# First token tiles of a fused attention and expert kernel: zeros stored later, experts prepared before the first keys, kv products and query copies a tile or two on

## Chip, cores and metric

The kernel runs on one core of a Trainium2 chip. The metric is the device time of one execution in microseconds (us), with the median of several runs as the value. Before the change the median of 3 runs is 1384.82 us.

## What is computed

Three layers follow each other on 4608 tokens of 512 values (8 batches of 576 tokens, 8 heads of 64): a linear attention with a root mean square norm, a mixture of 8 experts of which each token uses one, and a layer with a cosine gate. All of it is float32.

```python
kv = np.einsum('bhsd,bhse->bhde', k, v)
out = np.einsum('bhsd,bhde->bhse', q, kv)
rms = np.sqrt(np.mean(out * out, axis=-1, keepdims=True) + 1e-06)
x = (out / rms * g_norm)                       # then (4608, 512)
xn = x / (norm(x) + 1e-06); en = expert_emb / (norm(expert_emb) + 1e-06)
logits = xn @ en.T / tau                       # argmax picks the expert
out[mask] = gate_w[mask, None] * (np.maximum(x[mask] @ w1[e], 0.0) @ w2[e])
h = out @ w_in                                 # second layer
y = (h * np.cos(h)) @ w_out
```

## The kernel before

The order of the instructions on each engine is the order in which the code is written: there is no planner. Three stages run one after the other. The first, some 146 us long, makes the attention in 36 tiles of 128 tokens, finds each token's expert and scatters the rows to the expert's place in DRAM. The second runs the experts in chunks of 304 tokens, the third the last layer in blocks of 512 tokens. Only the first stage is touched.

**Loads.** SP's queue loads, batch by batch, `km`, `vm` (1 MB each), their remainders `kr`, `vr` and the queries `qm` (`load_kv`, `load_q`, L520 to L542). ScalarE's queue loads the embeddings, the temperature and the gain twice: `g2` by partitions and `g_bc` as a row on all partitions (L557 to L561). Behind them it stores four blocks of zeros, `none`, to columns 304 to 511 of `yT` (L581, 104 KB each). VectorE squares the gain row in place (L597); that step stands ahead of the steps of `prepare_experts` on VectorE. The loads share eight completion semaphores in turn: a load waits until the transfer that had its semaphore before is complete.

**A batch's kv.** `kv_pair(b, hp)` multiplies keys and values of two heads (L650, L653), with the copy to `kvb` after the fourth pair (L657). `kv_transpose` turns the four results on TensorE and copies them (L665, L667). `kv_logits` multiplies them by `gz`, the normed expert embeddings, and copies 16 columns per pair beside them (L673, L677). `prepare_experts` makes `gz` (L620 to L637): square, root and scaling of the embeddings on ScalarE and VectorE, four transposes on TensorE (L634).

**A tile.** `emit_out(t)` multiplies the turned queries `qT` by `kvb` (L706) and `emit_square(t)` squares the result on ScalarE (L716). `emit_root(t - 1)` takes a logarithm and an exponential of the tile before (L722, L723). `q_by_rows(b, half)` copies half of a batch's queries in another order on ScalarE (L616), and `emit_qT(t + 2)` turns the queries of the tile after the next on TensorE (L694) and copies them on ScalarE (L696); there is one PSUM buffer for that. Then come the kv steps of later batches that the tables `due_first` (tiles 0 to 8) and `due` name, in which (1, "t") is the transpose and (1, "z") the logits of the next batch but one half, and last the scaling on VectorE (L757). A batch has 4.5 tiles: tiles 0 to 3 are batch 0, 4 to 7 batch 1, and tile 8 holds the remainders of both.

**Spins.** `spin(n)` runs n products of a matrix of ones into an unused PSUM tile (L855), each in two instructions, to keep TensorE at work.

Of the kernel before, what the change touches and what calls it, by code (L numbers as in the profile page):

```python
# [19 lines left out]
B, H, S, D = 8, 8, 576, 64  # L20
# [5 lines left out]
NTILE = NT // 128  # L26
# [3 lines left out]
CH = 304  # L30
# [6 lines left out]
def tile_kernel(ctx, tc, q, k, v, g_norm, emb, tau, w1, w2, w_in, w_out, out):  # L37
    nc = tc.nc
# [6 lines left out]
    yT = dram.tile([DM, NT + CH], F32, name="yT")  # L45
# [450 lines left out]
    if True:  # L496
# [80 lines left out]

        none = ca.tile([128, 512 - CH], F32, name="none")
        nc.gpsimd.memset(none, 0.0)
        for d in range(4):  # L580
            nc.scalar.dma_start(out=yT[d * 128:(d + 1) * 128, CH:512], in_=none)  # L581
        nums = ca.tile([128, 4, 9], I32, name="nums")
        nc.gpsimd.iota(out=nums[:, :, 0:8], pattern=[[2 * S, 4], [S, 2], [1, 4]], base=0, channel_multiplier=4)
        for i in range(2):
# [57 lines left out]
        def kv_pair(b, hp):  # L642
            if hp == 0:
                kvp_t[b] = ps_s.tile([128, 4, 128], F32, name="kvp", tag="kvp")
            p, dst = kvp_t[b], kvb[b % 3]
            rr = slice(32 * (b % 4), 32 * (b % 4) + 32)
            ho = [(2 * hp + n, p[64 * n:64 * n + 64, hp, 0:D]) for n in range(2)]
            for r in range(4):
                for h, o in ho:
                    nc.tensor.matmul(out=o, lhsT=km[b][:, h, r, :], rhs=vm[b][:, h, r, :], start=(r == 0), stop=False)  # L650
            for r in range(2):
                for h, o in ho:
                    nc.tensor.matmul(out=o, lhsT=kr[rr, h, r, :], rhs=vr[rr, h, r, :], start=False, stop=(r == 1))  # L653
            if hp == 3:
                for n in range(2):
                    r = slice(64 * n, 64 * n + 64)
                    nc.scalar.activation(out=dst[r, :, n * D:(n + 1) * D], in_=p[r, :, 0:D], func=ACTF.Copy)  # L657
# [24 lines left out]
        def where(t):  # L682
            j, i = divmod(t, 9)
            return j, (2 * j + i // 4 if i < 8 else None), i % 4
# [168 lines left out]
        def spin(n):  # L853
            for i in range(n):
                nc.tensor.matmul(out=warm[:, 0, 0:128], lhsT=ones, rhs=ones, start=True, stop=True)  # L855

        spin(24)
        load_kv(1)
        load_q(1)
        load_kv(2)  # L860
        for hp in range(2):
            kv_pair(0, hp)
        prepare_experts()
        kv_pair(0, 2)
        q_by_rows(0, 0)
        kv_pair(0, 3)
        spin(5)
        emit_qT(0)
        spin(4)
        emit_qT(1)  # L870
        kv_transpose(0)
        q_by_rows(0, 1)
        spin(5)
        kv_logits(0)
        spin(2)

        due = {0: [(1, 2), (1, 3)], 1: [(1, "t")], 2: [(1, "z")], 3: [(2, 0), (2, 1)], 4: [(2, 2)], 5: [(2, 3)], 6: [(2, "t")],
               7: [(2, "z")], 8: [(3, 0), (3, 1)]}
        due_first = {**due, 0: [(1, 0), (1, 1)], 1: [(1, 2), (1, 3)], 2: [(1, "t")], 3: [(1, "z"), (2, 0)], 4: [(2, 1)],
                     5: [(2, 2), (2, 3)]}  # L880

        def advance(k):
            while k:
# [17 lines left out]
        for t in range(NTILE):  # L901
            j, b, r = where(t)
            paused.clear()
            if t == 0 or t % 9 in (2, 7):
                b0 = 2 * j + (1 if t else 0) + (t % 9 == 7)
                if b0 + 2 < B:
                    load_q(b0 + 2)
                load_kv(b0 + 3)
            todo = [(2 * j + d, what) for d, what in (due if t >= 9 else due_first)[t % 9] if 2 * j + d < B]
            po = ps_o.tile([128, 4, 256], F32, name="po", tag="po")  # L910
            cur["po"], cur["t"] = po, t
            emit_out(t, po)
            emit_square(t)
            if t >= 1:
                emit_root(t - 1)
            for half in range(2):
                tn = t + 4 - 2 * half
                if tn < NTILE and tn >= 4 and where(tn)[1] is not None and where(tn)[2] == 0:
                    q_by_rows(where(tn)[1], half)
            if t + 2 < NTILE:  # L920
                emit_qT(t + 2)
            for bb, what in todo:
                if what == "t":
                    kv_transpose(bb)
                elif what == "z":
                    kv_logits(bb)
                else:
                    kv_pair(bb, what)
            for it in ranking:
                next(it)  # L930
            mid += ranking
            ranking.clear()
            for x in TURNS.get(t, ()):
                turn_first(x)
            emit_x(t)
            advance(1)
            if late and late[0][0] <= t:
                split_piece(*late.pop(0)[1])
            if t in FIRST:
                late.append((FIRST[t][1], load_piece(FIRST[t][0])))  # L940
            if t == 29:

                kctx.close()
                rings.append(pool("ring1", 1, bctx, side="right"))
                P.xr.append(pool("xr1", 1, bctx, side="right"))
                P.xt = pool("xt", 2, bctx, side="right")
                P.h = pool("h", 3, bctx, side="right")
                P.gs = pool("gs", 2, bctx, side="right")
# [131 lines left out]
    if True:  # L1080
# [180 lines left out]
        for i in range(NB * 8 + 2):  # L1261
            b, q_ = divmod(i, 8)
# [164 lines left out]
```

## Time and profile before

| | before |
|---|---|
| median of 3 runs | 1384.82 us (1384.63 to 1391.18) |
| profiled execution | 1379.33 us |
| its span, first to last instruction | 1377.8 us |
| mean granted TensorE clock | 0.991 of 2.4 GHz |
| TensorE busy, weight loads busy | 97%, 90% of the span |
| VectorE, ScalarE, GpSimd busy | 73%, 50%, 13% |
| read and written in DRAM | 241.42 and 48.47 MB |

The profile shows one execution. Times are from the first instruction on. PE is TensorE and PEld its weight loads, DVE is VectorE, ACT ScalarE, POOL GpSimd; a q behind the name is the queue of transfers that the engine issues. In brackets stands how long the engine had been idle and what ended it. A clock of 1.00 is 2.4 GHz, 0.50 is 1.2 GHz.

### The profile page before, as it was taken

The numbers are of one execution on the slowest core, as the hardware profiler recorded it, in microseconds if no ns is written. First come the engines' busy times: TensorE is split into PE (matmuls) and PEld (weight loads), VectorE is DVE, ScalarE is ACT, GpSimd is POOL, SyncE is SP. The second block draws the span as 40 slices with busy tenths as digits, with TensorE's granted clock in tenths as the row PEclk, the third lists the DMA queues.
The fourth block names the chain that finished last, engine by engine and source line by source line (L and its number), as shares of the span: only waits on it lengthen the run. The fifth ranks groups of instructions, "written<-read, shape, count | busy, mean of one in ns | idle before, by whom it ended". The sixth has DMA issues, their size and how long they took to land. (4 is left out here: it accounts for less than half of the span.)

```text
span 1377.8 us, 26459 instructions
## 1 busy us (share of the span) xinstructions
PE 1342.7 (97%) x9545; PEld 1246.7 (90%) x9545; DVE 1002.1 (73%) x2287; ACT 688.9 (50%) x1297; POOL 176.6 (13%) x305
## 2 busy tenths in 40 slices
PE   8998899999999999999999999999999999999996
PEld 7886799999999999998898889888988898889885
DVE  1567967988888787878877676776767767676663
ACT  3667445555555454346555454554545455455442
POOL 1244132432222000000010100101001010000101
PEclk8999999999999999999999999999999999999999
DMA  9998486977877787389665756656566575655630
GB/s 271 294 330 256 138 241 183 268 233 237 242 231 243 217 221 205 110 277 342 196 207 185 233 167 200 219 178 222 175 211 211 161 240 183 204 192 181 215 118 33
DMA packets 197746, 291.73 MB, mean 212 GB/s; under 512 B 23036, under 2 KB 105504, under 8 KB 196392
## 3 DMA queue, kind: packets, MB, share of 16 engines
q1 hardware_dynamic: 178872, 224.82, 53.2%
q0 software_dynamic: 17824, 64.66, 14.5%
q8 instruction: 78, 1.28, 0.4%
q10 hardware_dynamic: 912, 0.48, 0.1%
q14 instruction: 60, 0.49, 0.1%
HBM read 241.42 MB, written 48.47 MB: 210 GB/s over the span
## 5 line engine op out<-in xcount | busy, mean ns | idle before, releaser
L1239 PE MATMUL o<-ring,g 128*128 128x512 f32 x1728 | 414.6, 395 | 0.0
L1239 PEld LDWEIGHTS o<-ring,g 128*128 128x128 f32 x1728 | 319.5, 188 | 72.7
L238 PE MATMUL hps<-xT,ring 128*128 128x304 f32 x1536 | 241.3, 306 | 2.3 <-DVE xT L227 1.2
L255 PE MATMUL y<-h,ring 128*128 128x304 f32 x1536 | 235.1, 302 | 0.8 <-DVE yo L263 0.8
L238 PEld LDWEIGHTS hps<-xT,ring 128*128 128x128 f32 x1536 | 219.7, 189 | 3.5 <-DVE h L245 1.5
L255 PEld LDWEIGHTS y<-h,ring 128*128 128x128 f32 x1536 | 220.0, 188 | 1.4 <-issue 1.3
L1127 ACT ACTIVATE n<-h 128x512 int32<-128x512 f32 x144 | 90.8, 632 | 115.8 <-DVE h L1164 112.8
L1133 ACT ACTIVATE u<-u,half_pi 128x512 f32<-128x512 f32 x144 | 103.4, 718 | 76.0 <-DVE u L1130 75.6
L1251 POOL DMA_INDIRECT out<-o_sb,perm_i x36 | 36.5, 1013 | 768.0 <-ACT o_sb L1250 625.6
L1164 DVE TENSOR_TENSOR h<-one,p 128x256 f32<-128x256 f32 x144 | 60.6, 421 | 90.5 <-ACT one L1196 79.0
L1169 DVE TENSOR_TENSOR u<-u,h 128x512 f32<-128x512 f32 x144 | 99.6, 692 | 29.3 <-ACT u L1133 29.2
L244 ACT ACTIVATE h<-hps 128x304 fp32r<-128x304 f32 x128 | 53.5, 418 | 108.9 <-PE hps L238 106.9
L1147 PEld LDWEIGHTS p<-ring,wa 128*128 128x128 f32 x840 | 103.2, 191 | 2.2 <-DVE one L1164 0.6
L1147 PEld LDWEIGHTS p<-ring,wb 128*128 128x128 f32 x840 | 103.2, 191 | 1.7
L1147 PE MATMUL p<-ring,wa 128*128 128x256 f32 x840 | 104.0, 283 | 0.4 <-DMA wa<-ws 0.4
L1147 PE MATMUL p<-ring,wb 128*128 128x256 f32 x840 | 103.7, 282 | 0.0
L142 DVE TENSOR_TENSOR ring<-raw,ring 128x1024 fp32r<-128x1024 f32 x72 | 87.8, 1219 | 15.3 <-ACT ring L141 13.3
L1178 DVE TENSOR_TENSOR g<-u,g 128x512 fp32r<-128x512 f32 x144 | 92.6, 683 | 0.1
L1130 DVE SCALAR_TENSOR_TENSOR u<-h,n 128x512 f32<-128x512 f32 x144 | 92.5, 682 | 0.0
L245 DVE SCALAR_TENSOR_TENSOR h<-hps,h 128x304 fp32r<-128x304 f32 x128 | 59.8, 467 | 42.7 <-ACT h L244 40.8
L1164 DVE TENSOR_TENSOR one<-one,p 128x256 f32<-128x256 f32 x72 | 30.3, 420 | 74.3 <-PE p L1147 74.3
L1196 ACT ACTIVATE one<-p 128x256 f32<-128x256 f32 x72 | 27.4, 381 | 113.4 <-PE p L1147 113.4
(229 smaller groups left out, 1823.0 us busy)
## 6 DMA issues: line engine op xcount, KB each, us to landing
wa<-ws SPq DMA_DIRECT2D x252, 256.0 KB
wb<-ws SPq DMA_DIRECT2D x252, 256.0 KB
raw<-in_moe_w SPq DMA_DIRECT2D x144, 256.0 KB
ws<-wa POOLq DMA_DIRECT2D x56, 256.0 KB
xr<-xs POOLq DMA_DIRECT2D x16, 627.0 KB
km<-in_k SPq DMA_DIRECT2D x8, 1024.0 KB
vm<-in_v SPq DMA_DIRECT2D x8, 1024.0 KB
qm<-in_q SPq DMA_DIRECT2D x8, 1024.0 KB
```

What stands on the lines that cost most here:

```text
L142: nc.vector.tensor_tensor(out=w[:, 1], in0=raw, in1=w[:, 0].bitcast(F32), op=ALU.subtract)
L238: nc.tensor.matmul(out=p[:, 0:CH], lhsT=w[:, a, k * 128:(k + 1) * 128], rhs=c["xT"][b_][k], start=(n == 0), stop=(n == 11),)
L245: V.scalar_tensor_tensor(out=lo, in0=p[:, 0:CH], scalar=0.0, in1=hi.bitcast(F32), op0=ALU.max, op1=ALU.subtract)
L255: nc.tensor.matmul(out=c["y"][d][:, 0:CH], lhsT=w[:, a, 512 + d * 128:512 + (d + 1) * 128], rhs=h[b_], start=(f == 0 and i == 0), stop=(f ...
L1127: nc.scalar.activation(out=n, in_=p, func=ACTF.Copy, scale=TURN, bias=0.25)
L1130: V.scalar_tensor_tensor(out=u, in0=p, scalar=TURN, in1=n, op0=ALU.mult, op1=ALU.subtract)
L1133: nc.scalar.activation(out=u, in_=u, func=ACTF.Sin, scale=2 * math.pi, bias=half_pi)
L1147: nc.tensor.matmul(out=out, lhsT=w[:, wi, a, k * 128:(k + 1) * 128], rhs=x[xi][:, b_, k * 256:(k + 1) * 256], start=(n == 0), stop=(n == 5),)
L1164: V.tensor_tensor(out=out, in0=x, in1=y, op=ALU.add)
L1169: V.tensor_tensor(out=u, in0=u, in1=h, op=ALU.mult)
L1178: V.tensor_tensor(out=g_[1], in0=u, in1=g_[0].bitcast(F32), op=ALU.subtract)
L1239: nc.tensor.matmul(out=ob[b][t], lhsT=g_[a][:, t * 128:(t + 1) * 128], rhs=w[:, b_, m * 512:m * 512 + 512], start=(q_ == 0 and m == 0 and ...
```

## The change

The four stores of zeros leave ScalarE's queue at the start and are issued on SP's queue at the end of tile 24. `prepare_experts` moves ahead of the first kv products, between 20 and 10 spins, and the rest of the start is put in another order. In tiles 0 to 8 the kv steps of batches 1 and 2 stand one or two tiles later, with transpose and logits of one batch in the same tile (3 and 7). The query copies, which stood four and two tiles ahead of the batch's first tile, stand by a table, `rows_at`, two and one tile ahead for batch 1 and three and one ahead for the others.

```diff
-        for d in range(4):
-            nc.scalar.dma_start(out=yT[d * 128:(d + 1) * 128, CH:512], in_=none)
...
-        spin(24)
         load_kv(1)
         load_q(1)
         load_kv(2)
-        for hp in range(2):
+        spin(20)
+        prepare_experts()
+        spin(10)
+        for hp in range(4):
             kv_pair(0, hp)
-        prepare_experts()
-        kv_pair(0, 2)
         q_by_rows(0, 0)
-        kv_pair(0, 3)
-        spin(5)
+        spin(3)
+        kv_transpose(0)
+        spin(2)
         emit_qT(0)
-        spin(4)
+        kv_logits(0)
         emit_qT(1)
-        kv_transpose(0)
         q_by_rows(0, 1)
-        spin(5)
-        kv_logits(0)
-        spin(2)
...
-        due_first = {**due, 0: [(1, 0), (1, 1)], 1: [(1, 2), (1, 3)], 2: [(1, "t")], 3: [(1, "z"), (2, 0)], 4: [(2, 1)],
-                     5: [(2, 2), (2, 3)]}
+        due_first = {**due, 0: [], 1: [(1, 0), (1, 1)], 2: [(1, 2), (1, 3)], 3: [(1, "t"), (1, "z")], 4: [],
+                     5: [(2, 0), (2, 1)], 6: [(2, 2), (2, 3)], 7: [(2, "t"), (2, "z")]}
+        rows_at = {2: [(1, 0)], 3: [(1, 1)]}
+        for b in range(2, B):
+            for half in range(2):
+                rows_at.setdefault(b // 2 * 9 + b % 2 * 4 - (3, 1)[half], []).append((b, half))
...
-            for half in range(2):
-                tn = t + 4 - 2 * half
-                if tn < NTILE and tn >= 4 and where(tn)[1] is not None and where(tn)[2] == 0:
-                    q_by_rows(where(tn)[1], half)
+            for x in rows_at.get(t, ()):
+                q_by_rows(*x)
...
+            if t == 24:
+                for d in range(4):
+                    nc.sync.dma_start(out=yT[d * 128:(d + 1) * 128, CH:512], in_=none)
```

**TensorE at the start, before.** Names are output and inputs; `po<-ones` is a spin, `kvp<-vm,km` and `kvp<-vr,kr` a pair of heads, `qTp<-ident,en` the experts' transposes.

```order
L855 MATMUL po<-ones 128x128 x24
L650 MATMUL kvp<-vm,km 64x64 x8
L653 MATMUL kvp<-vr,kr 64x64 x4
L650 MATMUL kvp<-vm,km 64x64 x8
L653 MATMUL kvp<-vr,kr 64x64 x4
L634 MATMUL qTp<-ident,en 128x8 x4
L650 MATMUL kvp<-vm,km 64x64 x8
L653 MATMUL kvp<-vr,kr 64x64 x4
L650 MATMUL kvp<-vm,km 64x64 x8
L653 MATMUL kvp<-vr,kr 64x64 x4
L855 MATMUL po<-ones 128x128 x5
L694 MATMUL qTp<-ident,qa_296 128x128 x4
```

The same place in the changed kernel (line numbers are two lower there):

```order
L853 MATMUL po<-ones 128x128 x20
L632 MATMUL qTp<-ident,en 128x8 x4
L853 MATMUL po<-ones 128x128 x10
L648 MATMUL kvp<-vm,km 64x64 x8
L651 MATMUL kvp<-vr,kr 64x64 x4
L648 MATMUL kvp<-vm,km 64x64 x8
```

The experts' transposes now stand ahead of all the products of batch 0, with ten spins between.

**ScalarE from just before tile 0 to tile 1, before.** `qa<-qm` is a query copy, `sq` a square, `y` the root, `qT<-qTp` the copy of turned queries.

```order
L616 ACTIVATE qa_342<-qm 128x1024
L677 ACTIVATE kvb_150<-kvp 128x4x16
L716 ACTIVATE sq<-po 128x512
L616 ACTIVATE qa_372<-qm 128x1024
L696 ACTIVATE qT<-qTp 128x512
L716 ACTIVATE sq<-po 128x512
L722 ACTIVATE y<-ms,lneps 128x8
L723 ACTIVATE y<-y 128x8
L696 ACTIVATE qT<-qTp 128x512
```

Tiles 0 to 2 in the changed kernel:

```order
L694 ACTIVATE qT<-qTp 128x512
L714 ACTIVATE sq<-po 128x512
L720 ACTIVATE y<-ms,lneps 128x8
L721 ACTIVATE y<-y 128x8
L694 ACTIVATE qT<-qTp 128x512
L714 ACTIVATE sq<-po 128x512
L720 ACTIVATE y<-ms,lneps 128x8
L721 ACTIVATE y<-y 128x8
L614 ACTIVATE qa_445<-qm 128x1024
L694 ACTIVATE qT<-qTp 128x512
```

The first query copy of batch 1 (`qa_372` before, `qa_445` now) stood behind the square of tile 0; it now stands behind the square of tile 2, directly ahead of the copy of tile 4's turned queries.

**TensorE from tile 2 to tile 4, before.** `po<-kvb,qT` are a tile's outputs, `qTp<-ident,qa` the turned queries, `kvp<-ident,kvb` the transposed kv, `kvp<-gz,kvs` the logits.

```order
L706 MATMUL po<-kvb_150,qT 128x144 x4
L694 MATMUL qTp<-ident,qa_372 128x128 x4
L665 MATMUL kvp<-ident,kvb_151 128x128 x4
L706 MATMUL po<-kvb_150,qT 128x144 x4
L694 MATMUL qTp<-ident,qa_372 128x128 x4
L673 MATMUL kvp<-gz,kvs 128x16 x4
L650 MATMUL kvp<-vm,km 64x64 x8
L653 MATMUL kvp<-vr,kr 64x64 x4
L706 MATMUL po<-kvb_151,qT 128x144 x4
```

Tiles 3 and 4 there in the changed kernel:

```order
L704 MATMUL po<-kvb_150,qT 128x144 x4
L692 MATMUL qTp<-ident,qa_445 128x128 x4
L663 MATMUL kvp<-ident,kvb_151 128x128 x4
L671 MATMUL kvp<-gz,kvs 128x16 x4
L704 MATMUL po<-kvb_151,qT 128x144 x4
L692 MATMUL qTp<-ident,qa_498 128x128 x4
```

The transposed kv of batch 1 and its logits stood a tile apart; they now follow each other directly, ahead of the first tile of batch 1.

## Rows read from the trace of the kernel before

**Rows 1.** By stretch: busy us of PE, PEld, DVE, ACT, POOL (instructions); clock, DMA share, GB/s.

```profile
90.00:120.00 30.00, 27.60 (x345) 24.12 (x343) 18.88 (x75) 20.43 (x49) 12.82 (x31) 1.00 1.07 323
120.00:146.00 26.00, 18.52 (x180) 15.68 (x178) 23.30 (x63) 21.38 (x47) 7.47 (x18) 1.00 0.72 215
```

**Rows 2.** Order of time, first 25 us: start, us, engine, line, operation, idle and releaser.

```profile
1.30 7.86 PE L855 MATMUL po<-ones 128*128 128x128 f32 x48 [1.30 <-POOL ones L565]
...
6.63 2.51 ACTq L581 DMA_DIRECT2D yT<-none  x4
9.18 0.30 ACT L592 ACTIVATE near_i<-ones 128x1 int32<-128x1 f32 x2 [6.86 <-DMA g<-in_g_norm]
...
10.54 0.22 DVE L597 TENSOR_TENSOR g_bc<-g_bc 128x64 f32<-128x64 f32 x1 [0.47 <-DMA g_bc<-in_g_norm]
...
11.18 0.38 SPq L520 DMA_DIRECT2D qm<-in_q  x1
...
11.30 0.69 PE L650 MATMUL kvp<-vm,km 128*64 128x64 f32 x16 [2.13 <-DMA vm<-in_v]
...
12.41 0.47 DVE L631 TENSOR_SCALAR en<-embt,es 8x512 f32<-8x512 f32 x1
...
17.83 2.25 PE L855 MATMUL po<-ones 128*128 128x128 f32 x10
...
18.10 1.06 ACT L616 ACTIVATE qa<-qm 128x1024 f32<-128x1024 f32 x1 [6.81 <-DMA qm<-in_q]
19.06 0.75 ACT L657 ACTIVATE kvb<-kvp 64x256 f32<-64x256 f32 x2
...
23.25 0.96 PE L673 MATMUL kvp<-gz,kvs 128*128 128x16 f32 x8
...
24.59 1.19 PE L706 MATMUL po<-kvb,qT 128*128 128x144 f32 x8
```

**Rows 3.** Busy time in short stretches, as Rows 1: the granted clock's falls and returns.

```profile
12.80:13.00 0.20, 0.20 (x13) 0.20 (x10) 0.09 (x1) 0.00 (x0) 0.00 (x0) 0.64 0.08 10
...
19.60:19.80 0.20, 0.20 (x3) 0.20 (x3) 0.00 (x0) 0.20 (x1) 0.00 (x0) 0.79 1.12 358
...
33.20:33.40 0.20, 0.20 (x10) 0.13 (x7) 0.20 (x2) 0.00 (x0) 0.00 (x0) 0.84 1.13 358
...
40.00:40.20 0.20, 0.20 (x2) 0.20 (x2) 0.20 (x1) 0.20 (x1) 0.00 (x0) 0.59 1.05 328
...
146.50:147.00 0.50, 0.46 (x2) 0.46 (x3) 0.50 (x2) 0.00 (x0) 0.00 (x0) 0.50 0.42 127
...
149.00:149.50 0.50, 0.50 (x4) 0.50 (x4) 0.43 (x4) 0.47 (x2) 0.00 (x0) 0.61 0.00 0
```

**Rows 4.** Order of time, 30 to 32 us, ScalarE and TensorE.

```profile
30.16 1.06 ACT L616 ACTIVATE qa<-qm 128x1024 f32<-128x1024 f32 x1 [3.76 <-DMA qm<-in_q]
...
31.76 0.66 PE L694 MATMUL qTp<-ident,qa 128*128 128x128 f32 x4 [2.39 <-ACT qT L696]
```

**Rows 5.** Order of time at full clock, 45 to 49 us: TensorE, then ScalarE.

```profile
45.93 1.25 PE L706 MATMUL po<-kvb,qT 128*128 128x144 f32 x8
47.01 0.60 PE L694 MATMUL qTp<-ident,qa 128*128 128x128 f32 x4
47.54 0.69 PE L650 MATMUL kvp<-vm,km 128*64 128x64 f32 x16
...
48.53 0.69 PE L650 MATMUL kvp<-vm,km 128*64 128x64 f32 x16
...
47.21 0.60 ACT L716 ACTIVATE sq<-po 128x512 f32<-128x512 f32 x1 [1.10 <-PE po L706]
...
48.14 1.04 ACT L616 ACTIVATE qa<-qm 128x1024 f32<-128x1024 f32 x1
```

**Rows 6.** Order of time, TensorE, the outputs of tile 8.

```profile
54.31 1.20 PE L706 MATMUL po<-kvb,qT 128*64 128x144 f32 x16
```

**Rows 7.** Order of time, TensorE, the outputs of tile 33.

```profile
137.79 1.25 PE L706 MATMUL po<-kvb,qT 128*128 128x144 f32 x8 [1.73 <-DVE xg L757]
```

## Prediction

> **What bounds the kernel now.** I read first the busy times by stretch, then the first 60 us in order of time, the granted clock in short stretches, and last the end of the stage that the change touches. Only the attention stage, some 146 of 1377.8 us, is edited; what follows runs the same instructions, so a tile that comes a microsecond later makes the kernel a microsecond longer unless something in the stage takes the delay up. In the middle of the stage TensorE is busy 27.6 of 30 us and its own weight loads apart no engine over 20.4 [rows 1], so nothing there is left to catch up with; in the last 26 us it is busy 18.5 us and VectorE 23.3 [rows 1].
>
> The start is a chain of waits. ScalarE spends 6.63 to 9.14 us on issuing the four stores of zeros and only then turns to its first activation [rows 2]. TensorE runs 24 dummy products until 9.16, waits 2.1 us for the values of batch 0, and starts the kv products at 11.30 [rows 2]. Its clock then falls to the half level (1.2 of 2.4 GHz) at 12.9 and comes back at 19.7 [rows 3]. The query tile of batch 0, whose issue waits until 11.18, lands at 18.10, and from there copies, transposes and logits lead to tile 0 at 24.59 [rows 2]. The second loss is at tile 2: ScalarE stands 3.76 us before the copy of batch 1's queries, with the copy of a transposed tile queued behind, and TensorE idles 2.39 us until 31.76 [rows 4]. The half clock follows from 33.3 to 40.15 [rows 3].
>
> **The zeros.** The issue on ScalarE goes away (2.5 us). I cost it at nothing: ScalarE can square the embeddings earlier, but VectorE's next step, the square of the gain row (g_bc), waits for that row's load until 10.54, and the experts' chain stands behind it in order [rows 2]. The load is ahead of the zeros on ScalarE's queue and stays there. In the changed program the query load of batch 0 waits for the semaphore of an early small load instead of that of the values; this brings the query loads forward by up to 3.5 us (11.18 against 7 to 8, an estimate). Batch 0's queries then no longer gate tile 0, batch 1's land at some 27 instead of 30.2. At tile 24 SP issues the four stores behind the last query loads and ahead of the weight piece of tile 25, which is split six tiles later: 2.5 us of issue [rows 2] beside 18 us of room at 3 us a tile, cost nothing. SP's queue holds nothing that is wanted before; POOL is not passed by anything.
>
> **The experts first.** The normed embedding is ready at 12.41 + 0.47 = 12.9 in the kernel before, held by the gain row, and I see nothing that makes it earlier. There the four small transposes stood behind four heads' products and waited for nothing. Now they stand ahead of all products. TensorE's twenty spins end near 1.30 + 20/24 of 7.86 = 7.9 [rows 2], and it idles 5 us where it idled 2.1. Transposes until 13.6; ten spins, at 2.25 us for five at half clock [rows 2], until 18.1. The four products need 0.99 us each at full clock (47.54 to 48.53, [rows 5]), about 1.65 at half. When does the clock come back? After two idle stretches it came 8.4 us after TensorE resumed (11.30 to 19.7, 31.76 to 40.15), after the third, ahead of expert products, 2.9 us after (146.5 to 149.4) [rows 3]. Here dense spins run first, so I take it between: full from the end of the spins, products done at 22.1. If it came at 16.3 (the 2.9 row), they would be done at 21.2; if at 21.4 (8.4 us), at 23.4. The Trainium skill, page TensorE: Matmul & The Clock Gate, section "Part 1: The HAM clock gate", has it that the slow level is the default and that activity alone releases it. By that rule the spins would do their work early and the products would end at 21.2 and the sum below would be 3.3; the rows of the first stretch, where products and then spins ran at half level for 6.8 us, speak against counting on it.
>
> From the products' end: copy of kv 0.75 us, query copy 1.06 [rows 2], copy of the transposed kv 0.60 (as any 128x512 on ScalarE, [rows 5]), logits 0.96 [rows 2], of which the next transposes hide the copy back, and those transposes 0.5 [rows 5]: 3.95 us with some 0.1 us between steps. Tile 0 starts at 26.05 instead of 24.59: **+1.5 us**, ends +0.6 and +2.8.
>
> **Products and query copies a tile on.** Tiles 0 to 8 took 24.59 to 54.31, 29.7 us, with the idle and the half clock in them [rows 2, 6]. I walk the new order with 1.08 us an output, 0.53 a transposed tile, 0.99 a pair and ScalarE's 0.93 from square to query copy [rows 5]. Tile 0: tile 2's transposes wait for the second query copy, issued only after tile 1's transposed copy: 0.65 idle. Tile 1 and its two pairs run through. Tile 2: transposes of tile 4 stand directly behind, and need a copy that ScalarE starts after tile 2's square and tile 1's root: 0.93 + 1.04 and the passing on, 2.1 us idle, in place of the 2.4 of before. Then the two pairs. Tile 3: transposed kv and its logits back to back, with square, root, query copy, two 0.6 copies on ScalarE between: 2.15 us idle, and 0.4 more until tile 4. Before, they were a tile apart. Tile 7 merges batch 2's in the same way, 1.15 us without a query copy. From tile 0 to tile 8 that gives 30.5 us at full clock: **+0.8 us**.
>
> From tile 9 on the pairs stand as before; the query copies come one tile later and are still wanted a tile after. ScalarE has 20.4 us of work in 30 [rows 1], so I cost them at nothing; if that cover fails, an estimate is half a query copy, 0.5 us, in each of six batches, 3 us.
>
> **The clock inside the tiles.** An idle of 2.4 us at 29.4 was followed by the half level for 6.8 us [rows 3, 4]. The new 2.1 and 2.55 us are about the same. One fall, after tile 2, costs: pairs 1.56 us of work at 1.65/0.99, output and transposes doubled, less the wait at tile 3 that this shortens: +1.9 us. Ends: no fall, 0; a fall after each of the two, +5. I take one, **+1.9 us**, since both idles lie about where the rows say falls happen and the second is smaller once the first has slowed TensorE.
>
> Sum: 1.5 + 0.8 + 1.9 = +4.2 us. The profiled execution took 1379.33 us (span 1377.8 and 1.5 around it), so 1383.5 by its own measure. The median of the three runs shown is 1384.82, 5.5 above; on it the forecast is **1389.0 us**.
>
> **Rivals.** *The gain row lands early (faster).* If g_bc lands sooner without the zeros, the experts come 2.35 us after it, and tile 0 moves one for one. At 6.0 us they are ready at 8.4, spins end at 11.7, products at 15.7, tile 0 at 19.65, or -4.9; with +0.8 and +1.9 this is -2.2 us, 1382.6. Without the fall of the clock, 1380.7. The point of no change is a landing 4.2 us earlier, at 6.3. For it: before, ScalarE's first activation waited for small loads of the same queue too [rows 2]. Against it: the gain row's step itself waited 0.47 us for the load until 10.54 [rows 2], and what is ahead of the row on its queue stays. 10%.
>
> *Two falls and a half-speed start (clearly slower).* Start +2.8, order +0.8, clock +5: +8.6, 1393.4. It decides if the products run at half clock to 21.4 and both idles are followed by a fall; for it the two early falls in the rows, against it the recovery after 2.9 us. A gain row that lands later adds to the same side, a microsecond for each: the query and key loads now follow the first ones without the wait until 11.18 [rows 2]. The Trainium skill, page DMA: Bandwidth & Descriptors, section "Queues, rings and completion order", says that a completion lands only after the earlier writes of that DMA engine, in whatever queue; by that rule the row could land later as the loads grow denser. No row here shows it apart. 20%.
>
> *The delay is taken up (no change).* At the end of the stage TensorE waits for VectorE's scaling of a tile, 1.73 us before 137.79 [rows 7], and in all 7.5 of the last 26 us are idle [rows 1]. If VectorE's backlog there came from weight pieces by the clock of their loads, late tiles would find it shorter and up to 4 us would vanish: 1385. Against it: the pieces stand in tile order, so they move along. Or the earlier loads hide what I count at tile 2. 22%.
>
> **Numbers.** Forecast 48%. A measurement tells some 0.5% (6.9 us) from no change: below 1377.9 or above 1391.7. Faster beyond it only if the gain row is early and nothing else is lost: 0.03. Slower: 17 of the 20 points and 2 of the forecast's own: 0.19. The rest, 0.78, within. The range reaches from the early row without a fall (1381) to above the two falls (1395).
>
> **What would show it.** Right: VectorE's g_bc step again near 10.5, TensorE idle from 8 to 13, tile 0 near 26, idles of 2 us before tile 4's transposes and before the logits at tile 3, tile 8 near 58, the rest shifted by the same. Wrong: experts' transposes before 11, tile 0 before 24.6, or a tile 30 that starts when it did.

## Result and profile after

| | before | after |
|---|---|---|
| median of 8 runs each | 1385.66 us (1382.65 to 1391.18) | 1394.56 us (1389.83 to 1399.64) |
| ratio of after to before | | 1.0065, 95% interval 1.0043 to 1.0087 |
| profiled execution | 1379.33 us | 1397.5 us |
| its span | 1377.8 us | 1396.0 us |
| mean granted clock of that execution | 0.991 | 0.984 |

The changed kernel is slower by 8.9 us. The two profiled executions are 18.2 us apart, because the profile of before is of one of its quickest executions and that of after of one of its slowest. So I read from the traces where time went, and from the medians how much.

The start of the changed kernel in order of time, first TensorE, then VectorE and SP's queue:

```profile
1.30 6.54 PE L853 MATMUL po<-ones 128*128 128x128 f32 x40 [1.30 <-POOL ones L565]
13.57 0.56 PE L632 MATMUL qTp<-ident,en 8*128 8x8 f32 x4 [5.73 <-DVE en L629]
14.06 4.64 PE L853 MATMUL po<-ones 128*128 128x128 f32 x20
18.62 0.73 PE L648 MATMUL kvp<-vm,km 128*64 128x64 f32 x16
...
22.64 0.94 PE L853 MATMUL po<-ones 128*128 128x128 f32 x6
...
26.79 1.24 PE L704 MATMUL po<-kvb,qT 128*128 128x144 f32 x8
...
11.08 0.23 DVE L595 TENSOR_TENSOR g_bc<-g_bc 128x64 f32<-128x64 f32 x1 [6.25 <-DMA g_bc<-in_g_norm]
...
6.49 0.32 SPq L527 DMA_DIRECT2D vr<-in_v  x1
6.85 0.45 SPq L520 DMA_DIRECT2D qm<-in_q  x1
```

The gain row's step stands at 11.08 (10.54 before, [rows 2]) and now shows as a wait of 6.25 us, since VectorE is done with all else at 4.8. TensorE idles 5.73 us, the products end at 22.64, and tile 0 stands at 26.79: 2.20 us later.

Tiles 2 to 8 of the changed kernel on TensorE, with the idles before turned queries (L692) and logits (L671):

```profile
32.58 1.25 PE L704 MATMUL po<-kvb,qT 128*128 128x144 f32 x8
35.89 1.12 PE L692 MATMUL qTp<-ident,qa 128*128 128x128 f32 x4 [2.06 <-ACT qa L614]
40.28 2.29 PE L704 MATMUL po<-kvb,qT 128*128 128x144 f32 x8
...
45.60 1.48 PE L671 MATMUL kvp<-gz,kvs 128*128 128x16 f32 x8 [2.05 <-ACT kvs L665]
47.40 2.29 PE L704 MATMUL po<-kvb,qT 128*128 128x144 f32 x8 [0.31 <-ACT kvb L675]
...
62.02 1.07 PE L671 MATMUL kvp<-gz,kvs 128*128 128x16 f32 x8 [1.21 <-ACT kvs L665]
63.71 2.19 PE L704 MATMUL po<-kvb,qT 128*64 128x144 f32 x16
```

Three idles, each from the step that stands ahead of it in the new order. The outputs of tile 3 and of tile 4 take 2.29 us, against 1.25 at full clock. The granted clock there (busy us of PE, PEld, DVE, ACT, POOL; clock, DMA share, GB/s), around each fall and return; all windows between a fall and its return are at 0.50:

```profile
18.50:19.00 0.50, 0.50 (x11) 0.38 (x12) 0.00 (x0) 0.00 (x0) 0.00 (x0) 0.73 1.12 358
35.50:36.00 0.50, 0.11 (x1) 0.11 (x2) 0.42 (x3) 0.34 (x1) 0.00 (x0) 0.83 1.05 181
42.50:43.00 0.50, 0.50 (x6) 0.50 (x5) 0.00 (x0) 0.39 (x1) 0.00 (x0) 0.84 1.10 348
46.00:46.50 0.50, 0.50 (x5) 0.50 (x5) 0.22 (x2) 0.00 (x0) 0.00 (x0) 0.57 1.14 170
52.50:53.00 0.50, 0.50 (x4) 0.41 (x2) 0.24 (x1) 0.50 (x2) 0.00 (x0) 0.60 1.15 282
63.00:63.50 0.50, 0.50 (x5) 0.50 (x4) 0.00 (x0) 0.22 (x1) 0.00 (x0) 0.64 1.03 335
```

With each of the three idles the half level comes, at its end or within 1.2 us of it: from 35.8 to 42.7, 46.1 to 52.9, and 63.1 to 66.6. Before, there was one such stretch between tile 0 and tile 8, of 6.8 us [rows 3], and I had put the idle ahead of it in the wrong tile. The 2.39 us of [rows 4] stand behind the outputs of tile 1, before the transposes of tile 3. The transposes of tile 4 come a tile later and had no idle; the outputs of tiles 1 and 2 and those transposes, before:

```profile
28.13 1.25 PE L706 MATMUL po<-kvb,qT 128*128 128x144 f32 x8
...
35.01 2.29 PE L706 MATMUL po<-kvb,qT 128*128 128x144 f32 x8
37.09 1.06 PE L694 MATMUL qTp<-ident,qa 128*128 128x128 f32 x4
```

So the 2.06 us before the transposes of tile 4 are a new idle, and not the old one in another form. Tile 8 now stands at 63.71 against 54.31 [rows 6], 9.40 us later. From there the stage keeps its distance: tile 9 is 10.84 us later, tile 27 11.14, tile 33, at 148.07 against 137.79 [rows 7], 10.28. In 90 to 120 us TensorE is as busy as in [rows 1]:

```profile
30.00:60.00 30.00, 25.57 (x281) 22.85 (x281) 12.30 (x43) 14.07 (x34) 1.14 (x6) 0.77 1.11 284
...
90.00:120.00 30.00, 27.84 (x344) 24.18 (x344) 19.06 (x75) 18.92 (x47) 12.23 (x31) 1.00 1.06 328
```

The remaining 8 us of the 18.2 come by 200 us. From 146 us on this execution has 13.7 us at half level, the one of before 3.4, which makes some 5 us; and TensorE waits 3.0 us longer for rows of the first chunk:

```profile
153.32 0.77 PE L221 MATMUL kvp<-ident,xr 76*128 76x76 f32 x4 [3.56 <-DMA xr<-xs]
```

Before, it was 0.54 us there. From the product that counts the experts' rows (L975) on, both take 1195 us more (200.85 to 1396.0, and 182.31 to 1377.8). How much half level lies between 146 and 200 us differs widely among the profiles below, from none to 17 us, whatever the tables.

**A measure over all executions.** Every execution has a span and a mean granted clock. Span times clock is about what it would have taken at full clock, and span times (1 - clock) what the half level added. This overstates the second where TensorE idled at half level. In the groups of runs of experiments 1 to 11, the kernel before had means of 1367.2 to 1368.8 and 16.3 to 16.7 us over 29 to 35 executions each. The changed kernel has 1374.0 and 19.2 over its eight: **some 6 us more at full clock, 2.6 us more by the clock.** The first is known to some 1.5 us either way (95%), the second to some 2.4. For the experiments the two differences to before in the same group of runs are called work and clock; there work is known to 0.7 to 1.5 us, clock to 1.6 to 3.9.

### The profile page after: what moved, and what is told of

Same layout as the page of the kernel before. It is cut to its first block, busy times and chain, and to the rows that moved or that the text cites. A ratio compares the mean times of both kernels' runs of the same rounds, so it can differ in the third digit from the quotient of the medians.

```text
span 1396.0 us, 26445 instructions
## 1 busy us (share of the span) xinstructions
PE 1350.7 (97%) x9535; PEld 1252.7 (90%) x9535; DVE 1002.7 (72%) x2287; ACT 689.5 (49%) x1297; POOL 177.2 (13%) x305
## 4 chain that ended last, share of the span: by engine, by line
PE 58%; DMA 0%; DVE 0%; issue 0%; ACT 0%; POOL 0%; POOLq 0%; DVEq 0%
PE o L1239 29%; PE p L1147 25%; PE y L255 2%; PE hps L238 2%; DMA wa<-ws 0%; ACT gx L175 0%; PE xp L221 0%; DVE gx L181 0%; POOL out L1251 0%; DVE h L245 0%; DVE o_sb L1248 0%; ACT c_mk L301 0%; DVE c_t L304 0%; DVE yo L263 0%; ACT h L244 0%
```

## Experiments

The first question was which part loses the time. My theory: the tables, and most of it by the clock. The rivals: the start, the zeros, or late tiles that are taken up again.

**1. The zeros alone.** The kernel before, with only the stores of zeros moved.

```diff
-        for d in range(4):
-            nc.scalar.dma_start(out=yT[d * 128:(d + 1) * 128, CH:512], in_=none)
...
+            if t == 24:
+                for d in range(4):
+                    nc.sync.dma_start(out=yT[d * 128:(d + 1) * 128, CH:512], in_=none)
```

> The kernel before with one edit: the four stores of zeros move from ScalarE's queue at the start to SP's at tile 24; start and tables as before. Theory (the harm is in the order of the start and of tiles 0 to 8, the zeros are harmless): batch 0's queries land some 3 us earlier than 18.1 and batch 1's some 3 us earlier than 30.2, so the 2.4 us idle at tile 2 and the half clock after it go or shrink; tile 0 at 22.5 to 24.6, tile 8 at 49 to 54, time 3 to 7 us below the kernel before (1379 to 1383). Rival (the zeros at tile 24 disturb the last loads, the scatter or the semaphores): tile 8 is no later than before, but time is lost after tile 24, 3 to 9 us above (1389 to 1395).

Measured: 1383.54 us, ratio 0.9993 (0.9967 to 1.0018); work -1.0, clock +0.2. No difference, and not the 3 to 7 us less that I expected. The outputs of tiles 0 and 1 and the transposes of tile 3, and then ScalarE's copy of batch 1's queries:

```profile
27.99 1.18 PE L704 MATMUL po<-kvb,qT 128*128 128x144 f32 x8
...
31.53 1.25 PE L704 MATMUL po<-kvb,qT 128*128 128x144 f32 x8
32.61 0.60 PE L692 MATMUL qTp<-ident,qa 128*128 128x128 f32 x4
...
30.21 1.06 ACT L614 ACTIVATE qa<-qm 128x1024 f32<-128x1024 f32 x1 [0.40 <-DMA qm<-in_q]
```

Batch 1's queries land no earlier than before (30.21 against 30.16, [rows 4]). Tile 0 is 3.40 us later (27.99 against 24.59), so that TensorE no longer waits for them: the idle of 2.39 us is gone, and tile 8 stands at 54.51, where it stood before. An idle of 0.69 us in tile 3, before the transposes of tile 5, is another one; the expectations below that speak of a wait of 0.7 us before tile 4's transposes take the two for one. Why the start is late is taken up in 8 and 12. The issue on SP beside tile 24 took 2.26 us in the changed kernel, in a stretch in which TensorE is as busy as before:

```profile
112.99 2.26 SPq L938 DMA_DIRECT2D yT<-none  x4
```

**2. The old start.** The changed kernel with the start of before.

```diff
-        spin(20)
-        prepare_experts()
-        spin(10)
-        for hp in range(4):
+        spin(24)
...
+        for hp in range(2):
             kv_pair(0, hp)
+        prepare_experts()
+        kv_pair(0, 2)
...
```

> The changed kernel with the start of the kernel before (24 spins, two pairs, experts, two pairs), zeros and tables as changed. Theory: the experts ahead of the products cost 2.2 us at tile 0 (26.79 against 24.59) and tables the rest; tile 0 at 22.5 to 24.6, the idles of 2 us at tiles 2 and 3 stay and the clock falls after at least one; tile 9 at 62 to 67 instead of 68.9, time 2 to 5 us below the changed kernel (1389.5 to 1392.5). Rival (the start carries most of it, because its long idle starts the row of clock falls): no falls in tiles 2 to 8, tile 9 at 58 to 60, time 8 to 10 below the changed kernel (1385 to 1387).

Measured: 1392.66 us, ratio 1.0043 (1.0017 to 1.0070); work +3.4, clock +3.1. Most of the loss stays, so the new start is not its main source: against the kernel of 1, which has the same start and the old tables, it is 0.50%. With the late zeros the old start is no better: tile 0 at 28.25, where I had expected 22.5 to 24.6.

**3. Both old tables.** The changed kernel, new start and late zeros, with the kv steps and query copies at the tiles of before.

```diff
-        due_first = {**due, 0: [], 1: [(1, 0), (1, 1)], 2: [(1, 2), (1, 3)], 3: [(1, "t"), (1, "z")], 4: [],
-                     5: [(2, 0), (2, 1)], 6: [(2, 2), (2, 3)], 7: [(2, "t"), (2, "z")]}
-        rows_at = {2: [(1, 0)], 3: [(1, 1)]}
-        for b in range(2, B):
+        due_first = {**due, 0: [(1, 0), (1, 1)], 1: [(1, 2), (1, 3)], 2: [(1, "t")], 3: [(1, "z"), (2, 0)], 4: [(2, 1)],
+                     5: [(2, 2), (2, 3)]}
+        rows_at = {}
+        for b in range(1, B):
             for half in range(2):
-                rows_at.setdefault(b // 2 * 9 + b % 2 * 4 - (3, 1)[half], []).append((b, half))
+                rows_at.setdefault(b // 2 * 9 + b % 2 * 4 - (4, 2)[half], []).append((b, half))
```

> The changed kernel with the kv tables and the places of the query copies of the kernel before; the new start and the zeros at tile 24 stay. Theory (tables carry most): tile 0 stays near 26.8, no idle over 1 us before tile 4, no fall of the clock after the start, tile 9 at 53 to 59 instead of 68.9, time 9 to 14 us below the changed kernel (1381 to 1386). Rival (the start carries it): tile 9 at 64 or later, time within 4 us of the changed kernel.

Measured: 1384.33 us, ratio 0.9987 (0.9961 to 1.0012); work +1.9, clock -3.7. The whole loss is gone, as the theory had it. Its TensorE, the outputs of tile 0, the transposes of tile 5 and the outputs of tile 8:

```profile
27.31 1.24 PE L704 MATMUL po<-kvb,qT 128*128 128x144 f32 x8
...
39.06 0.66 PE L692 MATMUL qTp<-ident,qa 128*128 128x128 f32 x4 [0.69 <-ACT qT L694]
...
53.04 1.20 PE L704 MATMUL po<-kvb,qT 128*64 128x144 f32 x16
```

From tile 0 to tile 8 it takes 25.73 us at full clock, where the kernel before took 29.72 [rows 2, 6]. The idle of 2.39 us [rows 4] is gone here without any move of the copies, as tile 0 comes 2.72 us later than before and ScalarE copies batch 1's queries at 29.42 without a wait. The largest idle left in these tiles is the 0.69 us.

**4. The idles filled.** The changed kernel with dummy products, into the PSUM tile of the next outputs, in the three idles.

```diff
+            if t == 2:
+                fill(t, 8)
...
+                    if t in (3, 7):
+                        fill(t, 8 if t == 3 else 4)
                     kv_logits(bb)
```

> The changed kernel with dummy products put into its three idle stretches: 8 ahead of tile 4's turned queries at tile 2, 8 ahead of the logits at tile 3, 4 ahead of those at tile 7 (about 0.25 us each at full clock). The waits for ScalarE stay as long as they are. Theory (most of what tiles 2 to 9 lose is the half clock after the idles, not the idles): granted clock 1.00 from 20 us on, tile 9 at 61 to 64 instead of 68.9, time 5 to 8 us below the changed kernel (1387 to 1390). Rival (the waits themselves are the loss, the clock matters little): tile 9 at 67 or later, time within 2 us of the changed kernel or above it.

Measured: 1385.38 us, ratio 1.0007 (0.9985 to 1.0028); work +8.1, clock -7.4. Below the range that I expected. The tiles come as late as the idles make them, with no half level from 20 us to 210:

```profile
27.52 1.24 PE L704 MATMUL po<-kvb,qT 128*128 128x144 f32 x8
...
34.39 1.95 PE L906 MATMUL po<-ones 128*128 128x128 f32 x16
36.62 0.66 PE L692 MATMUL qTp<-ident,qa 128*128 128x128 f32 x4 [0.28 <-ACT qa L614]
...
43.47 1.07 PE L671 MATMUL kvp<-gz,kvs 128*128 128x16 f32 x8 [0.37 <-ACT kvs L665]
...
58.65 1.20 PE L704 MATMUL po<-kvb,qT 128*64 128x144 f32 x16
```

Twenty products that compute nothing take 0.58%, some 8 us, off the changed kernel. They save no idle; what they save is the clock that was lost behind it: against the changed kernel work is 1 to 2 us more and clock some 10 us less.

**5 and 6. One old table at a time.** The changed kernel with the old kv steps (5), or with the old places of the query copies (6): the first or the second half of the diff of 3.

> The changed kernel with the kv steps of batches 1 and 2 back at the tiles of before; the query copies stay at the later places. My theory: each table makes its own idle and its own fall of the clock, and the two add up to the 10 us between the changed kernel (1394.6) and the one with both old tables (1384.3). Here the wait of some 2.1 us before tile 4's transposes stays, with one stretch of half clock of some 7 us behind it; the waits at tiles 3 and 7 go. Tile 8 at 56 to 59 us in the trace (53.0 with both old tables, 63.7 in the changed kernel) and 1387 to 1391 us. Rival: the falls come only from two idles close to each other; then this kernel loses no more than the bare 2 us and stands at 1384 to 1387, with no half clock between tile 2 and tile 8.

> The changed kernel with the query copies back four and two tiles ahead; the kv steps of batches 1 and 2 stay at the later tiles. My theory: the wait before tile 4's transposes shrinks to under 0.8 us and no clock falls there; the waits before the logits stay, some 2.1 us at tile 3 and 1.2 at tile 7, with one stretch of half clock behind the first. Tile 8 at 56 to 59 us and 1386 to 1390 us; with the kernel with old kv steps the two losses against both old tables add up to about 10 us. Rival: the falls come only from two idles close to each other; then 1384 to 1387 and no half clock between tile 2 and tile 8.

Measured: with old kv steps 1391.19 us, ratio 1.0025 (1.0007 to 1.0042), work +4.3, clock -0.6; with old copies 1390.33 us, ratio 1.0022 (1.0007 to 1.0037), work +4.7, clock -1.1. (Before stands at 1386.65 on this chip.) Against the 0.9987 with both, one table costs 0.38% and the other 0.35%; together 0.73%, and the changed kernel lies 0.78% above. Within the intervals, of some 0.3% each, they add. The rival, that it takes two idles close to each other, falls with the trace of 5: one new idle, and half level from 39.1 to 49.4. In that trace:

```profile
37.92 0.66 PE L692 MATMUL qTp<-ident,qa 128*128 128x128 f32 x4 [2.06 <-ACT qa L614]
...
58.95 1.60 PE L704 MATMUL po<-kvb,qT 128*64 128x144 f32 x16
```

and in the one with the old copies:

```profile
40.74 1.06 PE L671 MATMUL kvp<-gz,kvs 128*128 128x16 f32 x8 [1.22 <-ACT kvs L665]
...
55.41 1.06 PE L671 MATMUL kvp<-gz,kvs 128*128 128x16 f32 x8 [2.16 <-ACT kvs L665]
56.86 1.61 PE L704 MATMUL po<-kvb,qT 128*64 128x144 f32 x16
```

The 2.06 us are the query copy's and stay when only the kv steps are put back; the waits before the logits are the kv table's. Two things I had wrong: the longer idle of 2.16 us is at tile 7 and the 1.22 us at tile 3, since with the old places a query copy stands in tile 7 and none in tile 3; and in this execution only the longer one was followed by a fall, at 57.5, behind the start of tile 8.

**7. The gain row's step behind the experts'.** The changed kernel with the square of `g_bc` moved on VectorE.

```diff
-        nc.vector.tensor_tensor(out=g_bc, in0=g_bc, in1=g_bc, op=ALU.mult)
...
         prepare_experts()
+        nc.vector.tensor_tensor(out=g_bc, in0=g_bc, in1=g_bc, op=ALU.mult)
```

> The changed kernel with the square of the gain row moved on VectorE behind the steps that prepare the experts; everything else as changed. My theory: the gain row's load alone holds the experts; their transposes come at 7.8 to 9 us instead of 13.6, the ten spins end near 11, TensorE idles until the values' remainders land near 13, the products run at half clock and end near 20, tile 0 stands at 24 to 25.5 (26.8 in the changed kernel) and the tables' loss stays: 1391 to 1393.5 us. Rival 1: the shorter idle keeps the clock up, products end near 17, tile 0 at 21 to 22.5: 1388 to 1391. Rival 2: something else than the gain row holds the experts too (embeddings, temperature, gain by partitions); transposes stay above 12 us and the time at 1394 to 1396.

Measured: 1388.56 us, ratio 1.0024 (1.0000 to 1.0048); work +3.7, clock 0.0. Against the changed kernel that is 0.4% less, by 2.1 us of work and 2.6 of clock.

```profile
7.44 0.41 PE L631 MATMUL qTp<-ident,en 8*128 8x8 f32 x4
...
12.25 0.69 PE L647 MATMUL kvp<-vm,km 128*64 128x64 f32 x16 [1.97 <-DMA vr<-in_v]
...
32.37 0.66 PE L691 MATMUL qTp<-ident,qa 128*128 128x128 f32 x4 [2.06 <-ACT qa L613]
...
39.22 1.06 PE L670 MATMUL kvp<-gz,kvs 128*128 128x16 f32 x8 [2.16 <-ACT kvs L664]
...
54.40 1.20 PE L703 MATMUL po<-kvb,qT 128*64 128x144 f32 x16
```

The gain row alone held the experts: their transposes stand at 7.44 instead of 13.57, and tile 0 at 23.28. The time is that of rival 1, but not for its reason: the clock did fall, from 14.8 to 21.6. In this execution the idles of 2.06 and 2.16 us were followed by no fall before tile 8. So it shows the new order at full clock: 31.12 us from tile 0 to tile 8, as in the kernel of 4 (31.13), against 25.73 with the old tables in 3. **At full clock the new order costs 5.4 us.**

**8. Values first and experts early, old tables.** The kernel of 3 with the edit of 7, and the temperature loaded on GpSimd's queue, which leaves a completion semaphore free for the values' remainders.

```diff
-        nc.scalar.dma_start(out=taub, in_=tau.to_broadcast([E, 1]))
...
+        nc.gpsimd.dma_start(out=taub, in_=tau.to_broadcast([E, 1]))
```

> The kernel with both old tables, with the square of the gain row behind the experts' steps, and the temperature loaded on GpSimd's queue instead of ScalarE's, so that the values' remainders need not wait for the keys' transfer to be complete (their issue stood at 6.5 to 6.8 us without the zeros, at 3.6 before). My theory: experts' transposes at 7.8 to 9 us, products from 11.3 to 12 us, ended by 16 to 18.5, tile 0 at 20 to 22.5 (24.6 before, 27.3 with both old tables), tile 8 at 47 to 50 (54.3 before), no stretch of half clock after tile 0: 1378 to 1381 us, under both kernels. Rival: the loads of batch 1 set tiles 2 to 4, so that the earlier tile 0 is given back by tile 8 (52 to 54) and the time is 1382 to 1385.

Measured: 1387.25 us, ratio 0.9998 (0.9983 to 1.0014); work +0.6, clock -0.2. The theory fell. The remainders were issued at 4.10, but the products started at 13.40, waiting for `vm` itself; tile 0 stood at 25.24. Batch 1's queries landed at 31.25, a wait of 2.00 us before the transposes of tile 3 and a stretch at half level came with them, and tile 8 stood at 55.34.

**9. Batch 1's loads held back.** The kernel of 1, with a load of one value out of batch 0's values ahead of batch 1's keys, which SP can't issue before the values have landed.

```diff
         load_q(0)
+        held = ca.tile([1, 1], F32, name="held")
+        nc.sync.dma_start(out=held, in_=vm[0][0:1, 0, 0, 0:1])
```

> The kernel before with the zeros alone late (the one that measured 0.9993), plus a load of one value out of batch 0's values on SP's queue ahead of batch 1's keys, so that those cannot be issued before the values are there. My theory: without the zeros the transfers of batch 1 and the queries run beside batch 0's values, whose products then start at 13 instead of 11.3 us; held back, the products start at 10.8 to 11.8 again and tile 0 stands at 24 to 25, but the queries of batch 1 land later and the wait before tile 4's transposes (0.7 us without the hold, 2.4 before) is 1.5 us or more again: 1383 to 1388 us, no different from before. Rival: the values land late for another reason; products still start at 12.8 or later.

Measured: 1386.35 us, ratio 0.9998 (0.9986 to 1.0010). The time is the expected one, the reason is not: the products started at 13.41 although batch 1's keys were issued at 14.16. Nor did the wait for batch 1's queries come: they landed at 30.20, no later than in 1, and tile 0 stood at 27.99. What was still different from before was the query load at 7.05 and the remainders' at 6.68, and the latter alone had not helped in 8.

**10 and 11. Experts early, old tables, without and with fill.** The kernel of 3 with the edit of 7 (10), and with the eight dummy products behind tile 2 (11).

> The changed kernel's start and late zeros, with both old tables and the square of the gain row behind the experts' steps. My theory: transposes at 7.4 us, products at 12.3, tile 0 at 23.3 as with the new tables; with old tables tile 2 comes before batch 1's queries have been copied, so TensorE waits some 2 us there and in most executions a stretch of half clock follows; 1382 to 1386 us. Rival: the lead of 4 us at tile 0 over the kernel with both old tables (27.3) stays: 1379 to 1382.

> The same with eight dummy products in the wait behind tile 2's outputs. My theory: the wait is filled, no half clock between tile 0 and tile 9, tile 8 at 49 to 51 us (54.3 before) and 1380 to 1383.5 us, 1 to 4 us below the kernel without them. Rival: no difference between the two, because the clock does not fall there in most executions anyway.

Measured: 1387.90 us, ratio 1.0005 (0.9992 to 1.0017), and 1386.78 us, ratio 1.0013 (0.9994 to 1.0032). No gain over before; both lie above what I expected. The eight products of 11 missed their wait: they stand behind tile 2's outputs, while the wait (0.98 us) stands behind tile 1's, before the transposes of tile 3. So 11 does not tell what filling it is worth. In 10 tile 0 stands at 21.05 (21.01 in 11), earlier than in all other kernels; ScalarE's copy of batch 1's queries and TensorE around it:

```profile
24.43 0.69 PE L647 MATMUL kvp<-vm,km 128*64 128x64 f32 x16 [0.93 <-DMA vm<-in_v]
...
31.16 0.66 PE L691 MATMUL qTp<-ident,qa 128*128 128x128 f32 x4 [0.95 <-ACT qT L693]
33.73 1.25 PE L703 MATMUL po<-kvb,qT 128*128 128x144 f32 x8
...
29.57 1.06 ACT L613 ACTIVATE qa<-qm 128x1024 f32<-128x1024 f32 x1 [6.29 <-DMA qm<-in_q]
```

Batch 1's values land at 24.4 and its queries at 29.6, so of the 6.3 us that tile 0 was ahead of the kernel of 3, 1.5 are left at tile 2 (33.73 against 35.27). In these two kernels the first tiles are bound by the loads of two batches, though the experts come early. In the two profiles this is then lost again: both have 17 us at half level between 146 and 187 us, where that of 3 has none after 143.

**12. The queries held back.** The kernel of 1 with the edit of 8 and the load of one value ahead of batch 0's queries: the order of the first loads as it was before.

> The kernel before with the zeros alone late, and its order of the first loads put back: the temperature on GpSimd's queue, so that the values' remainders wait for nothing (issue at 4 us instead of 6.7), and the load of one value out of batch 0's values ahead of batch 0's queries, so that these are issued only after the values are there (11 instead of 7 us). My theory: the queries' transfer beside the values is what brought the first products from 11.3 to 12.2 to 13.4 us in the kernels with late zeros; here they start at 10.8 to 11.6, tile 0 stands at 24 to 25 and the wait before tile 4's transposes is 1.5 us or more, as before: 1383 to 1388 us, the same as before. Rival: the values land late for another reason that comes with the late zeros; products start at 12.2 or later, though no query load runs beside them.

Measured: 1381.30 us, ratio 1.0011 (1.0002 to 1.0019) against a before of 1380.9 on this chip. The first products, here and in the kernel of 1:

```profile
11.26 1.02 PE L650 MATMUL kvp<-vm,km 128*64 128x64 f32 x16 [2.78 <-DMA vm<-in_v]
```

```profile
12.97 0.69 PE L648 MATMUL kvp<-vm,km 128*64 128x64 f32 x16 [3.12 <-DMA vr<-in_v]
```

That is the start of before (11.30, [rows 2]) with the zeros late; tile 0 at 25.94 was a little later than expected, as the half level lasted from 11 to 22 us here. Of the two things put back, the earlier remainders had done nothing in 8, where the query load was issued at 6.79 and the products waited for `vm` until 13.40; here it is issued at 12.00. With 9, which rules out batch 1's loads, this points to the query load beside the values, which holds these up by 1 to 2 us (12.24 to 13.41 in the kernels with it), as far as one profile of each kernel can tell; a kernel with the queries held and nothing else put back was not run. The zeros had hidden it: before, SP waited 6.9 us for the values' own transfer ahead of the query load, and with the zeros gone it waits only 2.0 to 3.0 us, for the keys', before the remainders or the query load. That the four zeros did this by taking semaphores in turn is my reading of the program; no trace shows which transfer had which. The idle before tile 3's transposes is back as well, 1.70 us, with batch 1's queries landing at 30.82. No kernel of these beats the one before by more than its interval; the one with both old tables comes nearest.

## Why the prediction was right or wrong

The time, 1394.56 us, lies at the upper end of the range (1381 to 1395) and nearly on the rival that I called two falls and a half-speed start (1393.4, 20%), not on the forecast of 1389.0. The sum said +4.2 us; the runs say +8.9. A loss of 0.65% is beyond the 0.5% that I called no change, and I had given that 19%. That the time comes so near to the rival's is in part luck: its half-speed start did not come, and there were three falls and not two.

- **The start** (+1.5, ends +0.6 and +2.8): +2.20. The mechanism was right: gain row, 5.7 us idle, transposes near 13.6, full clock for the products. The clock came back at 18.7, at the end of the spins as I had it, and the products ended at 22.64 instead of 22.1, because all of it came half a microsecond later with the gain row. By the Trainium skill, page TensorE: Matmul & The Clock Gate, section "Part 1: The HAM clock gate", with activity alone releasing the clock, I had worked out 21.2; this trace is farther from that than from the row. A later gain row I had named as a risk. It stands at 10.90 to 11.53 in the kernels with an early query load, and at 10.27 with the queries held (10.54 before). That agrees with the Trainium skill, page DMA: Bandwidth & Descriptors, section "Queues, rings and completion order", by which a completion waits for the DMA engine's earlier writes; no run took the row by itself.
- **The zeros** (nothing): right, 0.9993. That the query load would come forward was right too (6.85), as was that batch 0's queries would no longer gate tile 0. Batch 1's queries I had at some 27 us, which is wrong: where ScalarE waited for them they landed at 29.5 to 31.3 (experiments 1 and 8 to 12), before at 30.16. What I did not see is that the early query load slows the values' own transfer (experiment 12), because their products now stood behind the experts anyway.
- **The order of tiles 0 to 8** (30.5 us at full clock): 31.1 in experiment 7. The idles were foretold at 2.1, 2.15 and 1.15 us, and are 2.06, 2.05 and 1.21.
- **The clock inside the tiles** (+1.9, upper end +5): **this is the step that failed, by size.** I took one fall for two idles of equal length, with the reason that the second is smaller once the first has slowed TensorE. It was 2.05 us all the same, since the clock was back at 42.7, before that idle began at 43.5; only in experiment 2, where the half level lasted through it, was it 1.33 us. And a third fall followed the 1.21 us of tile 7. In the profile tiles 0 to 8 take 36.92 us, so the clock costs 5.8 of them. Over all executions: my 29.7 us for tiles 0 to 8 before held 3.4 us of lost clock (6.8 us at half level), so the forecast meant +5.7 of work (1.5 + 0.8 + 3.4) and -1.5 of clock. Measured are about +6 and +2.6. So some four of the missing 4.7 us are the clock's, to some 2.4 us either way.
- **The query copies from tile 9 on** (nothing): right. Tiles 9 to 27 take 60.94 us, before 60.64.
- **The delay taken up at the end** (22%): no. Tile 33 is 10.28 us late where tile 8 was 9.40.
- **The idle that the later copies were to replace** ("in place of the 2.4 of before") was misplaced: the 2.39 us for the queries' landing [rows 4] stand before the transposes of tile 3, and those of tile 4 had no idle. The sum does not change by it, as I took the 29.7 us of before as measured. But the old idle goes with a later tile 0 alone (experiments 1, 3 and 9), so the later copies cured nothing, and they made an idle where there was none: the copy now stands behind the square of its own tile and the root of the tile before, directly ahead of the transposes that need it.

## What to carry to other kernels

When an order table is changed, price every new idle twice, for itself and for the stretch at half clock that may follow; here idles of 5.4 us cost 0.78% or 10.8 us, and dummy products in them gave 8 of it back. Transpose, copy and next product directly behind each other made TensorE wait for the copies here (2.05 and 1.21 us), so keep a tile between them. An idle that a load sets moves with the tiles ahead of it: here batch 1's queries landed at 29.5 to 31.3 us wherever ScalarE waited for them, and the idle for them was gone where tile 0 stood at 27.3 to 28.3 and there where it stood at 24.6 to 25.9. Before taking a few transfers out of a start, see whose semaphore the next loads then share: removing them can let a load go that had better wait.

## What the runs showed of the chip

- Nine idles of 2.0 to 2.4 us stand between tile 0 and tile 8 of the profiles at full clock (before, after twice, experiments 2, 5, 6, 7 twice, 8). With seven the half level came within some 2 us of their end, with the two of experiment 7 it did not. Of four idles of 1.2 us (after, experiments 2, 6, 7) two had it within 3 us, and in experiments 1, 9 and 10 it came behind idles of 0.69 and 0.45 us. So an idle's length alone tells a chance and no more; what decides stays open.
- A stretch at half level lasted between 3.4 and 13.7 us in the first 200 us of the fourteen profiles: of 57 stretches 27 lasted 3.4 us, 20 lasted 6.8, nine 10.2 and one 13.7 (before: 6.8, 6.8 and 3.4). So the price of one idle differs fourfold from case to case.
- In the executions of before the half level cost 16.5 us on average, with a standard deviation of 3.2 to 4.3 us, while the work varied by 1.5 to 2.1: most of the spread between executions is the clock. The stalls named "issue" near 191 to 196 us of the changed kernel, which come with it in that execution, were not explained.
